# A second visit with plain float32 scores, differences and splits on GpSimd, and free PSUM banks for the last gather

## The chip, the cores and the metric

The kernel runs on one core of a Trainium2 chip. TensorE (PE) multiplies matrices into PSUM; VectorE (DVE), ScalarE (ACT) and GpSimd (POOL) do elementwise work; SyncE (SP) issues the DMAs. The metric is the device time of one execution in microseconds (us), lower is better, given as the median of several runs. One further execution was taken by the profiler, and all rows come from it.

## What is computed

An attention in which each row sees only the rows of its own hash bucket, and a feed-forward layer on its output:

```python
q_bits = (einsum('bhsd,dk->bhsk', q, proj) > 0)      # 6 bits, k likewise
mask = q_bucket[:, :, :, None] == k_bucket[:, :, None, :]
scores = where(mask, 0.125 * q @ k.T, -1e9)          # B, H, S, D = 4, 8, 768, 64
attn = exp(scores - max) / (sum + 1e-9)
x = (attn @ v).transpose(0, 2, 1, 3).reshape(3072, 512)
out = maximum(x @ w_in, 0) ** 2 @ w_out              # w_in 512x2048, w_out 2048x512
```

## The kernel before, in words

The kernel has a fast and a general version; the fast one runs, checks its own assumptions (`verify`), and the general one is behind a branch that is not taken. All that follows is of the fast one.

Attention is cut into visits: a batch, a pair of heads and one half (384) of the queries. A visit has two times three units of 128 queries. A unit's scores go to PSUM (`pS`), VectorE evacuates them to `e` with the row's maximum, ScalarE takes the exponential with the row's sum, and the reciprocal `rv` of the sum is made from it. In the first four visits GpSimd divides (`e<-e,rv`), TensorE transposes into `pT`, and ScalarE or VectorE copies that to `aT`. In later ones ScalarE and VectorE write a high and a low float16 part (`hl`), and a DMA transposes them. `av` multiplies by the values into `pA`, and `xx` takes its high and low part.

Scores are usually made from operands that are stacked to 128 rows in float16: `prep` loads `R`, takes its high part `A` and low part `L`, and by ten DMAs for a pair of heads (`Q<-A`, `Q<-L`, `A<-A`, `L<-M`, `M<-Q`) stacks those with the hash codes `M`. The first visit does without: `first` and `side_by_side` take the loaded keys `K` and queries `G` in float32 on 64 rows of TensorE, and the codes `MK` and `MG` in float16, for both heads of the pair next to each other. `WIDE = 1` is the number of such visits.

The weights come as float64, are put together to float32 (`top`, `f`), and split into a high and a low float16 part (`win`, `wo`). When the four visits of a batch half are done, `moe` runs for it: eight times, each with 16 slices of the hidden layer. A slice is 12 matmuls into `pm`, a Relu and a square into `g32`, the high part and the difference to it (`left`) into `g`, and 9 matmuls into the three banks of `po`, where all 16 slices are gathered. At the end of a layer the three banks are moved to `o` and stored.

The order on each engine is not that of the code. `Program` notes all operations with their dependencies, and `order` plans forwards and backwards with a cost for each operation, which also decides for operations with several ways (`pr.add`) which engine takes it: the end on that engine plus its cost times `PRICE`. In `forward` a `port` that VectorE and GpSimd share is reserved (`held`) for the operations that the function `port` names. `region` tells which parts of a tile an operation touches; in PSUM that is a bank, and two readings of one bank count as dependent too. The instructions are then issued in the planned order, with semaphores that are set from the tiles.

Of the kernel before, what the change touches and what calls it, by code (L numbers as in the profile page):

```python
# [23 lines left out]
P = 128  # L24
# [14 lines left out]
    True: dict(xx=12, hl=3, f=3, e=4, aT=3, g=2, A=8, Q=8, L=8, M=8, R=2, VV=5),  # L39
    False: dict(xx=12, hl=3, raw=2, f=7, e=3, aT=3, g=2, A=2, Q=2, L=2, M=2, R=2, VV=6),  # L40
}
PRICE = dict(pe=1, dve=3.57, act=0.3, pool=3.06, sp=0.43)
AHEAD, DELAY, LAG = 60, 2500, 1.0

ROUNDS, BEHIND = 4, 40000
# [16 lines left out]

TOP_BY, LOW_BY = ("dve", "act"), ("dve", "pool")
RUN = 18
CONSTS_BY, WIDE = ("sp", "sp", "sp"), 1
CHECK_RANK, EARLY = 200, 24


# [61 lines left out]
class Program:  # L130
# [24 lines left out]
    @staticmethod  # L155
    def region(view):
        ap, rec = view.ap, view.rec
        size = lambda dims: 1 + sum(st * (n - 1) for st, n in dims)
        if rec.kind == "dram":
            return 0, 1, ap.offset, ap.offset + size(ap.ap), 0, 0, 0  # L160
        p0, f0 = divmod(ap.offset, rec.row)
        if rec.kind == "psum":
            return 0, 1, f0 // 512, 1 + (f0 % rec.row + size(ap.ap[1:]) - 1) // 512, 0, 0, 0

        (step, n), inner = ap.ap[1], size(ap.ap[2:])
        block = (step, f0 % step, f0 % step + inner) if n > 1 and f0 % step + inner <= step else (0, 0, 0)
        return (p0, p0 + ap.ap[0][1], f0, f0 + size(ap.ap[1:])) + block

    def add(self, *ways):


        ways = [w for w in ways if w[0].key != "pool" or not any(isinstance(x, View) and x.rec.kind == "psum" for x in w[2])]
        queue, name, args, kw = ways[0]
        if name == "matmuls":
            used = [(x, n == 0) for a, _ in args for n, x in enumerate(a)]
        else:
            used = [(args[0], True)] + [(x, False) for x in args[1:]] + [(x, k == "accum_out") for k, x in kw.items()]
        used = [(x.rec, w, self.region(x)) for x, w in used if isinstance(x, View)]
        i, deps = len(self.ops), set()
        for rec, w, (p0, p1, f0, f1, fs, g0, g1) in used:  # L180
            if rec.before is not None:
                deps |= rec.before.ops
            for j, w2, (a0, a1, b0, b1, bs, c0, c1) in rec.accesses:
                if (w or w2 or rec.kind == "psum") and a0 < p1 and p0 < a1 and b0 < f1 and f0 < b1 and not (fs and fs == bs and (c1 <= g0 or g1 <= c0)):
                    deps.add(j)
        for rec, w, r in used:
            rec.ops.add(i)
            rec.accesses.append((i, w, r))
        deps.discard(i)
        if self.mark is not None:  # L190
            self.paced.append((i, self.mark))
        self.ops.append(Op([w + (self.cost(w[0].key, *w[1:]), self.port(w[0].key, *w[1:])) for w in ways], deps, self.rank))

    @staticmethod
    def cost(key, name, args, kw):
# [3 lines left out]
        if name == "matmuls":  # L199

            side = {32: 4, 64: 2}.get(size(args[0][0][1]), 1)
            t = sum(size(a[2]) * column.get(a[2].dtype, 1 / 2.4) + 7 for a, _ in args) / side
            return t, t
        kinds = [x.rec.kind if isinstance(x, View) else "" for x in args]
        ptr = any(isinstance(x, View) and x.shape[-1] == 1 for x in args[2:3])
# [29 lines left out]
    def port(key, name, args, kw):  # L235
# [4 lines left out]
        inside = all(x.rec.kind == "sb" for x in ins)  # L240
        if key == "pool":
            return any(x.rec.kind == "sb" for x in args[1:] if isinstance(x, View) and len(x.shape) > 1 and x.shape[-1] > 1)
        return inside and (len(ins) == 2 or name in ("tensor_copy", "tensor_scalar"))

    def order(self):
        ops = self.ops
# [71 lines left out]
    def forward(self, prio, near):  # L318
# [5 lines left out]
        later = {k: [] for k in keys}  # L324
        ready = {k: [] for k in keys}
        free = dict.fromkeys(keys, 0.0)
        out, dma, dge, held, kind = [], 0.0, 0.0, 0.0, None

        def offer(i):
            for w in ops[i].ways:  # L330
# [8 lines left out]
        while True:  # L339
# [44 lines left out]
            if o.name.startswith("dma"):  # L384
# [4 lines left out]
                    o.busy = busy = dma + 467 - t  # L389
                dma += done  # L390
                done = dma + 910 - t
            free[k], o.end = t + busy, t + done
            out.append(i)
            for j in o.users:
# [54 lines left out]
def run(ctx: ExitStack, tc, kq, v, proj2, w_in, w_out, consts, out, flag):  # L449
# [56 lines left out]
    if fast:  # L506
# [5 lines left out]
        dve.memset(masks[T, 1:2], -65504.0)  # L512
        dve.memset(masks[U, 0:1], 2.0**16)
        dve.memset(masks[U, 1:2], 0.0)
        codes = sb([P, 4 * P], BF16, "codes")
        for t, x in enumerate((2.0 / BIG, 2.0)):
            for j in range(2):
                w = slice(2 * j, 2 * j + 2)
# [288 lines left out]
    def moe(n, b, half):  # L807
# [6 lines left out]
        for f in range(NF + 1):  # L814
# [23 lines left out]
            if f > 0:  # L838
# [2 lines left out]
                pr.mark = None  # L841
                first, last = (m % 4 == 0, m % 4 == 3) if grouped else (m == 0, m == NF - 1)
                if first:
                    po = ps([P, 3, DM], F32, "po")
                for t in range(3):
                    gh = g[:, 0, t * P : (t + 1) * P]
                    gl = g[:, 1, t * P : (t + 1) * P]
                    pr.rank, pr.mark = RANK_PE, pace()
                    pe.matmul(po[:, t], gh, wo[:, 0, m], start=first, stop=False)
                    pe.matmul(po[:, t], gh, wo[:, 1, m], start=False, stop=False)  # L850
                    pe.matmul(po[:, t], gl, wo[:, 0, m], start=False, stop=last)
                    pr.mark = None
                pr.rank = RANK_MOE
                if grouped and last:
# [3 lines left out]
                for t in range(3):  # L858
                    r0 = b * S + half * HS + t * P
                    if grouped and last:  # L860
                        if m == 3:
                            move(acc[:, t], po[:, t], back)
                        else:
                            dve.scalar_tensor_tensor(acc[:, t], po[:, t], back, acc[:, t], ALU.mult, ALU.add)
                        if m == NF - 1:
                            send(out[r0 : r0 + P], acc[:, t])
                    elif last:
                        o = sb([P, DM], F32, "o", tag="f")
                        move(o, po[:, t], back)
                        send(out[r0 : r0 + P], o)  # L870
            if n == 0 and f in (1, 5, 9):
                j = f // 4 + FIRST
# [160 lines left out]
```

## Time and profile before

| | |
|---|---|
| median of 3 runs | 832.88 us (832.54 to 834.76) |
| the profiled execution | 834.86 us, span 833.1 us |
| TensorE busy | 794.3 us (95%) |
| ScalarE busy | 656.6 us (79%) |
| VectorE busy | 605.2 us (73%) |
| GpSimd busy | 72.7 us (9%) |
| DMA, share of 16 engines | 77.2% |

A row of a timeline gives the start and the duration in us, the engine, the line, the operation with output and inputs by the program's names, and the shapes; in brackets the idle time of the engine just before, and what ended it. A matmul's duration holds its latency, so that the steps between starts tell what TensorE gets through. Every operation goes through one helper line, so all rows have L427 or L424, and names tell them apart.

### The profile page before, as it was taken

How to read it: one execution, taken by the hardware profiler on the slowest of the kernel's cores; microseconds unless marked ns; L12 is line 12 of the kernel's file. 1: busy time of each engine (PE TensorE's matmuls, PEld its weight loads, DVE VectorE, ACT ScalarE, POOL GpSimd, SP SyncE). 2: the span in 40 equal slices, each digit the busy share in tenths (PEclk: the TensorE clock that was granted, in tenths of full speed). 3: DMA queues.
4: the chain of work that ended last, by engine and by line, in shares of the span. 5: the costliest groups of instructions: out<-in, count | busy, mean ns of one | idle time of the engine just before them, and what ended most of it. 6: DMA issues, size and time to landing. Idle time of an engine off the chain costs nothing. (4 is left out here: it accounts for less than half of the span.)

```text
span 833.1 us, 14383 instructions
## 1 busy us (share of the span) xinstructions
PE 794.3 (95%) x5001; PEld 430.0 (52%) x5001; DVE 605.2 (73%) x1200; ACT 656.6 (79%) x1238; POOL 72.7 (9%) x175
## 2 busy tenths in 40 slices
PE   7797799999999999999999999999999999999996
PEld 4354355555555554555555545555555554555553
DVE  6888989998999888898879755888889433611110
ACT  5898999998888989888898856888988997334443
POOL 1255200100000010000000000000002000000000
PEclk9999999999999999999999999999999999999999
DMA  8985979999999999999989866988975889501001
GB/s 258 270 223 181 292 188 179 214 176 195 183 202 196 195 188 213 192 181 219 194 188 186 212 165 140 181 143 148 146 133 99 239 290 304 212 1 39 1 1 42
DMA packets 299521, 145.93 MB, mean 175 GB/s; under 512 B 268752, under 2 KB 279344, under 8 KB 299440
## 3 DMA queue, kind: packets, MB, share of 16 engines
q1 hardware_dynamic: 299440, 144.93, 77.2%
q8 instruction: 41, 0.67, 0.3%
q14 instruction: 40, 0.33, 0.1%
HBM read 56.80 MB, written 6.29 MB: 76 GB/s over the span
## 5 line engine op out<-in xcount | busy, mean ns | idle before, releaser
L427 PE MATMUL po<-wo,g 128*128 128x512 f16 x1152 | 296.9, 379 | 5.7 <-ACT o L427 5.7
L427 PE MATMUL pm<-xx,win 128*128 128x384 f16 x1536 | 297.7, 326 | 4.4 <-ACT g L427 2.8
L427 PEld LDWEIGHTS <-win 128*128 128x128 f16 x1536 | 149.9, 98 | 116.6 <-issue 8.0
L427 DVE TENSOR_SCALAR_CACHE_REDUCE e<-pS 128x768 f32<-128x768 f32 x192 | 182.7, 953 | 21.9 <-PE pS L427 17.7
L427 ACT ACTIVATE e<-e,maxes 128x768 f32<-128x768 f32 x192 | 178.2, 929 | 20.7 <-DVE e L427 19.2
L427 DVE SCALAR_TENSOR_TENSOR hl<-e,rv,hl 128x768 f16<-128x768 f32 x168 | 171.0, 1019 | 18.8 <-ACT hl L427 17.8
L427 PEld LDWEIGHTS <-g 128*128 128x128 f16 x1152 | 111.9, 98 | 124.8 <-issue 9.1
L427 ACT ACTIVATE hl<-e,rv 128x768 f16<-128x768 f32 x168 | 154.6, 923 | 6.0 <-DMA aT<-hl 5.2
L427 DVE SCALAR_TENSOR_TENSOR g<-g,g 128x384 f16<-128x384 f32 x121 | 66.9, 553 | 111.8 <-ACT g L427 111.4
L427 ACT ACTIVATE g<-g 128x384 f32<-128x384 f32 (+1 forms) x251 | 129.4, 517 | 6.6 <-PE po L427 2.7
L427 ACT ACTIVATE g<-pm 128x384 f32<-128x384 f32 x127 | 61.2, 482 | 90.3 <-PE pm L427 90.0
L427 PE MATMUL pS<-A,Q 128*128 128x384 f16 x372 | 93.1, 330 | 4.1 <-DVE e L427 2.6
L427 PE MATMUL pS<-L,M 128*128 128x384 f16 x372 | 91.8, 327 | 0.8 <-DMA M<-Q 0.8
L424 PE MATMUL pA<-aT,VV 128*64 128x384 f16 x1008 | 87.2, 327 | 0.0
L427 POOL TENSOR_SCALAR rv<-sums 128x1 f32<-128x1 f32 x136 | 36.8, 271 | 541.7 <-ACT e L427 400.2
L424 PEld LDWEIGHTS <-VV 128*64 128x64 f16 x1008 | 54.7, 110 | 32.9 <-issue 10.0
L427 PEld LDWEIGHTS <-Q 128*128 128x128 f16 x372 | 34.2, 98 | 43.1 <-issue 16.2
L427 DVE TENSOR_SCALAR M<-pc,masks 128x384 f16<-128x384 f32 x64 | 43.0, 672 | 15.4 <-PE pc L427 15.2
L427 PEld LDWEIGHTS <-M 128*128 128x128 f16 x372 | 36.3, 98 | 25.1 <-DMA M<-Q 1.2
L427 ACT ACTIVATION_READ_ACCUMULATOR e<-e,maxes 128x1 f32 x192 | 36.6, 191 | 0.0
L427 DVE SCALAR_TENSOR_TENSOR L<-R,A 128x768 f16<-128x768 f32 x32 | 30.4, 950 | 7.7 <-ACT A L427 7.5
L427 PE MATMUL pT<-unit_f,e 128*128 128x128 f32 x144 | 23.8, 293 | 10.5 <-ACT aT L427 7.7
(82 smaller groups left out, 517.4 us busy)
## 6 DMA issues: line engine op xcount, KB each, us to landing
R<-kq SPq DMA_DIRECT2D x32, 384.0 KB, 3.8
X<-kq SPq DMA_DIRECT2D x32, 384.0 KB, 4.1
raw<-w_in SPq DMA_DIRECT2D x16, 511.8 KB, 5.6
raw<-w_out SPq DMA_DIRECT2D x16, 511.8 KB, 4.9
V<-vp SPq DMA_DIRECT2D x20, 384.0 KB, 5.1
out<-o SPq DMA_DIRECT2D x24, 256.0 KB, 2.7
X<-vp SPq DMA_DIRECT2D x16, 384.0 KB, 4.4
Q<-L SPq DMA_DIRECT2D x32, 96.0 KB, 2.9
```

What stands on the lines that cost most here:

```text
L424: ins = q.engine.matmul(*map(real, args), **kw).ins
L427: ins = getattr(q.engine, o.name)(*map(real, o.args), **{k: real(x) for k, x in o.kw.items()}).ins
```

## The change

- `WIDE = 2`: the first visits of two head pairs use `first` and `side_by_side`. Their stacked operands are needed only for the other query half, four visits later.
- `PRICE` of ScalarE goes from 0.3 to 1, of GpSimd from 3.06 to 1.5, so GpSimd gets more of what it may take: differences, splits and high parts.
- The function `port` names for VectorE only `tensor_copy` and `tensor_scalar` inside SBUF, no longer operations with two SBUF inputs.
- The planner takes a PSUM tile as one region, and two readings as independent.
- The planner knows of eight DMA lanes (`LANES`): SP waits for the DMA eight before.
- TensorE's side-by-side products get a cost of their own.
- In the last of the eight layers `po` is two banks of the tile `pS` and one of `pA`, and the middle `o` of each layer is VectorE's.
- `codes` shares buffers with `g32`.

```diff
-PRICE = dict(pe=1, dve=3.57, act=0.3, pool=3.06, sp=0.43)
+PRICE = dict(pe=1, dve=3.57, act=1, pool=1.5, sp=0.43)
...
+LANES = 8
-CONSTS_BY, WIDE = ("sp", "sp", "sp"), 1
+CONSTS_BY, WIDE = ("sp", "sp", "sp"), 2
...
         if rec.kind == "psum":
-            return 0, 1, f0 // 512, 1 + (f0 % rec.row + size(ap.ap[1:]) - 1) // 512, 0, 0, 0
+            return 0, 1, 0, 1, 0, 0, 0
...
-                if (w or w2 or rec.kind == "psum") and a0 < p1 and p0 < a1 and b0 < f1 and f0 < b1 and not (fs and fs == bs and (c1 <= g0 or g1 <= c0)):
+                if (w or w2) and a0 < p1 and p0 < a1 and b0 < f1 and f0 < b1 and not (fs and fs == bs and (c1 <= g0 or g1 <= c0)):
...
             t = sum(size(a[2]) * column.get(a[2].dtype, 1 / 2.4) + 7 for a, _ in args) / side
+            if args[0][0][1].shape[0] == D and len(args) == 2:
+                t *= 0.5 if args[0][0][2].dtype == F32 else 0.7
...
-        return inside and (len(ins) == 2 or name in ("tensor_copy", "tensor_scalar"))
+        return inside and name in ("tensor_copy", "tensor_scalar")
...
                 done = dma + 910 - t
+                if k != "pool":
+                    lanes.append(t + done)
+                    if len(lanes) >= LANES:
+                        busy = max(busy, lanes[-LANES] + 60 - t)
...
-        codes = sb([P, 4 * P], BF16, "codes")
+        codes = sb([P, 4 * P], BF16, "codes", 2, tag="g32")
...
                 if first:
-                    po = ps([P, 3, DM], F32, "po")
+                    if fast and n == 2 * B - 1:
+                        po = ps([P, 2, 512], F32, "pS"), ps([P, 512], F32, "pA")
+                        po = [po[0][:, 0], po[0][:, 1], po[1]]
+                    else:
+                        po = ps([P, 3, DM], F32, "po")
+                        po = [po[:, t] for t in range(3)]
...
-                        move(o, po[:, t], back)
+                        move(o, po[t], back, (dve,) if fast and t == 1 else (act, dve, pool))
```

The order of instructions changes everywhere. Three places show how. First GpSimd's queue at the start, before: the sums' `rv` and the divisions of the first visit.

```order
L427 TENSOR_SCALAR rv_257<-sums_244 128x1 [waits Activation_49]
L427 TENSOR_SCALAR e_232<-e_232,rv_257 128x768 [waits DVE_49]
L427 TENSOR_SCALAR rv_283<-sums_244 128x1 [waits Activation_49]
L427 TENSOR_SCALAR e_246<-e_246,rv_283 128x768 [waits DVE_49]
L427 TENSOR_SCALAR rv_338<-sums_244 128x1 [waits Activation_49]
L427 TENSOR_SCALAR e_301<-e_301,rv_338 128x768 [waits DVE_49]
```

And the same place after:

```order
L434 TENSOR_SCALAR rv_198<-sums_192 128x1 [waits Activation_49]
L434 TENSOR_SCALAR e_184<-e_184,rv_198 128x768 [waits DVE_49]
L434 TENSOR_TENSOR win_201<-f_187,win_201 128x512 [waits Activation_49]
L434 TENSOR_SCALAR rv_246<-sums_192 128x1 [waits Activation_49]
L434 TENSOR_TENSOR win_201<-f_203,win_201 128x512 [waits Activation_49]
L434 TENSOR_TENSOR L_269<-R_144,A_251 128x768 [waits DMAHW4_49,Activation_49]
L434 TENSOR_SCALAR A_280<-R_190 128x768 [waits DMAHW2_49]
L434 TENSOR_SCALAR e_195<-e_195,rv_246 128x768 [waits DVE_49]
L434 TENSOR_SCALAR e_255<-e_255,rv_278 128x768 [waits DVE_49,Activation_49]
```

Between the first and the second division there are now two low parts of `w_in`, an `L` and an `A`.

Second, SP's queue, before, from its 17th entry: the first visit's `K` and `G` and the second's `R` are issued, and the stacking of the second visit begins (`Q_189`, `Q_221`).

```order
L427 DMA Q_189<-L_140 64x768 [waits DMAHW1_49,DVE_49]
L427 DMA R_195<-kq 128x768 [waits DMAHW2_49,PE_49,Activation_49]
L427 DMA Q_189<-A_97 64x768 [waits DMAHW3_49]
L427 DMA R_216<-kq 128x768 [waits DMAHW4_49,DVE_49,PE_49]
L427 DMA Q_221<-L_191 64x768 [waits DMAHW5_49]
L427 DMA Q_221<-A_173 64x768 [waits DMAHW6_49]
```

And after, from the 11th entry: the second visit's `K_157` and `G_165`, with the third visit's `R` around them.

```order
L434 DMA R_144<-kq 128x768 [waits DMAHW4_49]
L434 DMA unit_f_149<-consts 128x128 [waits DMAHW5_49]
L434 DMA K_157<-kq 64x768 [waits DMAHW6_49]
L434 DMA K_157<-kq 64x768 [waits DMAHW7_49]
L434 DMA G_165<-kq 64x384 [waits DMAHW0_49]
L434 DMA G_165<-kq 64x384 [waits DMAHW1_49]
L434 DMA R_190<-kq 128x768 [waits DMAHW2_49]
```

The second visit has four plain loads and no stacking; the first stacking DMA is ten entries later in the queue.

Third, TensorE at the end of the last layer, before: the gather of the last two slices, in one tile `po`.

```order
L427 MATMUL po_8985<-wo_460,g_9387 128x512
L427 LDWEIGHTS g_9365
L427 MATMUL po_8985<-wo_460,g_9365 128x512 [waits Activation_49]
L427 LDWEIGHTS g_9387
L427 MATMUL po_8985<-wo_460,g_9387 128x512
L427 LDWEIGHTS g_9387
L427 MATMUL po_8985<-wo_460,g_9387 128x512 [waits Activation_49]
```

And after, in the tiles `pS` and `pA`:

```order
L434 LDWEIGHTS g_9394
L434 MATMUL pS_8992<-wo_386,g_9394 128x512
L434 LDWEIGHTS g_9384
L434 MATMUL pA_9003<-wo_386,g_9384 128x512
L434 LDWEIGHTS g_9384
L434 MATMUL pA_9003<-wo_386,g_9384 128x512
L434 LDWEIGHTS g_9394
L434 MATMUL pA_9003<-wo_386,g_9394 128x512
```

The two waits for ScalarE's evacuations are gone from TensorE's queue; five matmuls into `pA` follow the last one into `pS`.

## Rows read from the trace of the kernel before

**Rows 1.** Busy us (x instructions) per engine in four stretches, then clock, DMA, GB/s.
```profile
0.00:97.70 97.70, 74.65 (x485) 43.33 (x485) 79.60 (x175) 80.62 (x162) 36.09 (x53) 0.97 0.83 242
97.70:655.00 557.30, 551.63 (x3586) 299.11 (x3586) 480.87 (x948) 481.71 (x878) 36.65 (x122) 1.00 0.90 181
655.00:819.00 164.00, 161.41 (x902) 84.62 (x900) 43.59 (x76) 90.37 (x193) 0.00 (x0) 1.00 0.39 126
819.00:833.10 14.10, 6.61 (x33) 2.92 (x30) 1.12 (x2) 3.88 (x8) 0.00 (x0) 0.86 0.17 62
```

**Rows 2.** TensorE's waits in 0 to 97.7: us in total, times, longest.
```profile
PE pT L427 <- ACT aT L427: 7.7, 8, 2.2
PE pc L427 <- ACT bits L427: 3.0, 2, 2.8
...
PE pS L427 <- DMA A<-A: 1.3, 1, 1.3
...
PE pS L427 <- DMA M<-Q: 0.8, 1, 0.8
```

**Rows 3.** TensorE's waits from 97.7 on.
```profile
PE po L427 <- ACT o L427: 5.7, 8, 0.9
PE pm L427 <- ACT g L427: 2.8, 5, 1.0
```

**Rows 4.** Timeline where the first stage ends, GpSimd and TensorE.
```profile
89.62 0.91 POOL L427 TENSOR_SCALAR e<-e,rv 128x768 f32<-128x768 f32 x1 [3.42 <-PE pT L427]
...
97.70 0.32 PE L427 MATMUL pm<-xx,win 128*128 128x384 f16 x1 [1.04 <-ACT xx L427]
```

**Rows 5.** Timeline of TensorE in the first visit.
```profile
6.78 1.55 PE L424 MATMUL pS<-K,G 64*128 64x384 f32 x4
...
22.14 1.56 PE L424 MATMUL pS<-K,G 64*128 64x384 f32 x8
23.53 0.49 PE L424 MATMUL pS<-MK,MG 64*128 64x384 f16 x4
23.95 0.85 PE L424 MATMUL pd<-R,pj 128*32 128x384 f32 x8
```

**Rows 6.** The chain that ended last: start us, us, what, in steps.
```profile
628.92 0.65 PE pS L427 x4
629.74 1.73 PE po L427 x8
```

**Rows 7.** By tile (`e`, `f`, `g`, `hl`): duration ns min/median/max, first and last start.
```profile
L427 POOL TENSOR_SCALAR e<-e,rv x24: 907/909/1468, 17.0 to 89.6; 128x768 f32<-128x768 f32 x24
...
L427 DVE SCALAR_TENSOR_TENSOR f<-raw,top x22: 671/684/876, 13.2 to 95.9; 128x512 uint32<-128x512 uint32 x22
...
L427 POOL TENSOR_TENSOR g<-g,g x7: 912/915/1041, 147.0 to 644.1; 128x384 f16<-128x384 f32 x7
...
L427 DVE SCALAR_TENSOR_TENSOR hl<-e,rv,hl x168: 998/1015/1706, 115.4 to 653.6; 128x768 f16<-128x768 f32 x168
```

**Rows 8.** Groups by form: busy us, mean ns of one, idle before and its releaser.
```profile
L427 DVE SCALAR_TENSOR_TENSOR L<-R,A 128x768 f16<-128x768 f32 x32 | 30.4, 950 | 7.7 <-ACT A L427 7.5
...
L427 POOL TENSOR_TENSOR win<-f,win 128x512 f16<-128x512 f32 x3 | 3.5, 1173 | 4.1 <-ACT win L427 4.0
```

**Rows 9.** Timeline of GpSimd and VectorE at 639.8.
```profile
639.80 0.92 POOL L427 TENSOR_TENSOR g<-g,g 128x384 f16<-128x384 f32 x1 [2.70 <-ACT g L427]
639.83 1.71 DVE L427 SCALAR_TENSOR_TENSOR hl<-e,rv,hl 128x768 f16<-128x768 f32 x1
```

**Rows 10.** Timeline of the end, TensorE and ScalarE.
```profile
824.90 0.81 PE L427 MATMUL po<-wo,g 128*128 128x512 f16 x3 [0.69 <-ACT o L427]
...
826.39 0.59 PE L427 MATMUL po<-wo,g 128*128 128x512 f16 x2 [0.69 <-ACT o L427]
827.02 0.60 ACT L427 ACTIVATE o<-po 128x512 f32<-128x512 f32 x1 [0.68 <-PE po L427]
```

**Rows 11.** Timeline of one slice in the last layer.
```profile
805.94 0.33 PE L427 MATMUL pm<-xx,win 128*128 128x384 f16 x1
...
807.94 0.56 DVE L427 SCALAR_TENSOR_TENSOR g<-g,g 128x384 f16<-128x384 f32 x1 [3.33 <-ACT g L427]
```

More of the change, by code (lines that the diff above doesn't have):

```diff
@@ L326, in forward @@
         free = dict.fromkeys(keys, 0.0)
-        out, dma, dge, held, kind = [], 0.0, 0.0, 0.0, None
+        out, dma, dge, held, kind, lanes = [], 0.0, 0.0, 0.0, None, []
         def offer(i):
@@ L848, in moe @@
                     pr.rank, pr.mark = RANK_PE, pace()
-                    pe.matmul(po[:, t], gh, wo[:, 0, m], start=first, stop=False)
-                    pe.matmul(po[:, t], gh, wo[:, 1, m], start=False, stop=False)
-                    pe.matmul(po[:, t], gl, wo[:, 0, m], start=False, stop=last)
+                    pe.matmul(po[t], gh, wo[:, 0, m], start=first, stop=False)
+                    pe.matmul(po[t], gh, wo[:, 1, m], start=False, stop=False)
+                    pe.matmul(po[t], gl, wo[:, 0, m], start=False, stop=last)
                     pr.mark = None
@@ L861, in moe @@
                         if m == 3:
-                            move(acc[:, t], po[:, t], back)
+                            move(acc[:, t], po[t], back)
                         else:
-                            dve.scalar_tensor_tensor(acc[:, t], po[:, t], back, acc[:, t], ALU.mult, ALU.add)
+                            dve.scalar_tensor_tensor(acc[:, t], po[t], back, acc[:, t], ALU.mult, ALU.add)
                         if m == NF - 1:
```

## The prediction

> **What bounds the kernel now.** I first read the busy time of the engines in four stretches [rows 1], because the share over the whole span averages stages with different limits. From 97.7 us on TensorE is busy 551.6 of 557.3 us and then 161.4 of 164.0 us: whatever other engines gain there is worth nothing unless a wait of TensorE goes. In the first 97.7 us it is busy 74.7 us, so 23 us are lost, while ScalarE (80.6) and VectorE (79.6) are the full ones and GpSimd (36.1) is not. That stretch ends when the fourth visit's attention output lets the first feed-forward matmul start, at 97.70 [rows 4]. Next come the waits of TensorE. Early ones are for the copies of transposed weights, for bits and for the DMAs that stack the second visit's operands [rows 2]; after 97.7 us the largest single item is `po` behind ScalarE's `o`, 5.7 us in 8 waits, then 2.8 us for `g` [rows 3]. So the time is: end of the first stage, plus TensorE's remaining work, plus its stalls, plus the end. The change is worth what it does to these four terms.
>
> **First stage, the second visit.** It gets float32 scores on 64 rows instead of stacked float16. Removed ahead of it: two of the four `pc` products, and the stacking DMAs for which TensorE waited 1.3 and 0.8 us; 3.0 us went to bits that stood before its scores in the queue [rows 2]. I count 4 of these 5.1 us as gained, 0 to 5.1 as bounds. Added to TensorE: a pair of units side by side took 1.81 us (22.14 to 23.95 [rows 5]), against 8 x 0.163 = 1.30 us for stacked ones [rows 6], 0.5 us each for two pairs. The visit's first pair runs one half after the other: four products at 1.55 / 2 us [rows 5] and four small ones at about 0.16 are 3.7 us, 2.4 us more. With three more `pd` (under 0.85 us, the four of [rows 5]) and three `pc` (0.163 each) that is 4.7 us. Its cover is the 23 us of idle TensorE; without the cover it costs all 4.7. Four new loads go on the SP queue and stand before the loads of the third visit; the stacking itself is not gone, it moves behind the fourth visit, where the same ten DMAs and M evacuations are issued.
>
> **First stage, GpSimd's share.** By program order, up to its 24th and last division GpSimd does 24 divisions and 4 low parts before, and now 24 divisions, 15 low parts, 6 `L` differences, 4 `A`, 1 `VV` and 10 high parts. Prices: division 0.909 [rows 7], low part 1.17 [rows 8]; an `L` is not in the trace, and from 0.915 us at 384 and 1.17 at 512 elements [rows 7, 8] the line goes to 1.67 at 768; high parts 0.909 x 512/768 = 0.61. That is 26.5 us before and 21.8 + 17.6 + 10.0 + 4.5 + 6.1 = 60.0 us after. VectorE's operations with two inputs in SBUF up to its fourth `xx`: before 22 `f`, 17 low parts (0.684 each [rows 7]), 8 `L` and 3 `VV` (0.95 [rows 8]), 37.1 us; after 26 `f`, 7 low parts, 2 `L`, 3 `VV`, 27.3 us. These two sums belong together, since such operations do not overlap: with GpSimd's difference at 639.80 running for 0.92 us, VectorE's `hl` of normally 1.015 us took 1.71 [rows 9, 7]. The pair ended after 1.74 us instead of the 1.94 us of its parts, 10% less. The port that they share thus has (26.5 + 37.1) x 0.9 = 57 us of work before, in the 77.3 us from the first `f` at 13.2 [rows 7] to the end of the last division, 89.62 + 0.91 [rows 4]; after, 87.3 x 0.9 = 78.6 us. So ScalarE and VectorE are relieved, but this port becomes full. At 95% of use, which I choose because TensorE, whose order is planned in the same way, keeps 99% where it is full [rows 1], it takes 82.7 us, 5.5 us more; less the 4 us above, +1.5 us. Bounds: -6 (two vector engines relieved, port no limit) to +10 (no overlap in pairs at all).
> The Trainium skill ("SBUF — State Buffer", Who interferes with whom) says that a VectorE instruction with two SBUF inputs and a GpSimd instruction that reads SBUF block each other wholly, whoever is first having the port. The row agrees but for the 0.2 us. By the row the port has 78.6 us of work, by the rule alone 87.3, and +1.5 would be +10.7.
>
> **What is left after it.** At the first feed-forward matmul the new order has one more unit's scores (4 x 0.163) and one more `pd` set (0.85 [rows 5]) behind it: 1.5 us less to follow.
>
> **Evacuations of the gather.** Before, in seven of the eight layers a later bank's matmul stands behind ScalarE's `o` of an earlier one, 0.69 us in the two waits of the last layer [rows 10]. In the new order no such wait stands inside a layer: all matmuls precede the first evacuation or use the other tile. Between layers 2.4 us or more of other matmuls (priced by [rows 6]) cover a chain of three evacuations of some 0.6 us [rows 10]; the last layer, where only 1.5 us stand there, gathers in banks that are free. I take 5.0 of the 5.7 us, bounds 3.0 to 5.7. In the end the last matmuls go to `pA` while two `o` are moved, and the last `o` and its store stay as they are.
>
> **Differences on GpSimd.** 117 `g` differences go from 0.56 us [rows 11] to 0.915 [rows 7]. In the last layers the difference starts at 807.94, 2.0 us after the last `pm` at 805.94 [rows 11], and would end at 808.9; the matmul that needs it stands 3.5 us of matmuls (12 `pm`, 7 `po` [rows 6]) behind, at 809.6: covered, and 0.7 us is left. Between 97.7 and 655 us the same distance is 4.5 to 6.8 us in the middle, but there VectorE's `hl` and `e` share the port: GpSimd's about 156 us in 557 meet 168 `hl` in some 47 places, at half of the 0.7 us of [rows 9] each, 16 us of delay on one of the two engines. Slack should take most: 1.5 us, bounds 0 to 8. Behind a late `hl` is the next `e` on VectorE, and behind that TensorE's `pS`.
>
> **Sum.** +1.5 - 1.5 - 5.0 + 1.5 = -3.5 us. The profiled execution took 834.86 us with a span of 833.1; it is 2 us over the median of 832.88, so I apply the difference to the median: 829.4 us. Its own bounds are 825 to 834.
>
> **Rivals.** First, the relief is real and the port is not the limit: the two full engines of the first stage lose about 8 us (VectorE: 6 `L` and 10 low parts less, 4 `f` and some `rv` more), and the stage ends 6 us earlier instead of 1.5 later: 822 us. For it speaks that GpSimd was idle for 62% of the stage; against it the pair in [rows 9]. Second, slower: the port binds fully. 87.3 us with no overlap at 95% use are 92 us in place of 77.3, less 4: +10.7 instead of +1.5, giving 839 us. It decides once demand on the port exceeds the 77 us; the new planner no longer sets the port aside for VectorE operations with two inputs, so nothing in the order avoids such meetings. The Trainium skill's rule ("SBUF — State Buffer", Who interferes with whom), taken literally, is this case. Third, GpSimd's differences come too late in the long stretch: half of the 16 us reaches TensorE, 8 instead of 1.5, 836 us; for it speak `rv` and `L` ahead of `g` in GpSimd's queue, against it the 4.5 us of distance. That the free banks change nothing, because the waits are replaced by others of the same length, is the low end of that term (3.0) and leaves 831.
>
> **Numbers.** Forecast 0.45, first rival 0.2, second 0.22, third 0.13. A measurement of this kernel can tell about 0.3% (2.5 us) from no change: faster means under 830.4, slower over 835.4. The forecast's span splits into 0.28 faster, 0.16 same, 0.01 slower, the third rival into 0.07 and 0.06; with the others faster 0.48, same 0.23, slower 0.29. The range 820 to 840 holds the forecast's own bounds, both middles of the first two rivals and all but their far halves.
>
> **What would show it.** The first `pm` near 99 us (92 in the first rival, 108 in the second); divisions on GpSimd well above 0.91 us in the mean; the wait of `po` for `o` under 1 us in total; `hl` well above 1.02 us in the mean, with few waits of TensorE for `g` or `e` after the first stage. I am wrong if GpSimd's slower `L` delays the third visit's stacks, if ScalarE is the stage's limit whatever the port does, or if TensorE's idle stretches early on bring the half clock, which the first stage showed only in part (0.97 [rows 1]).

## The result and the profile after

The changed kernel takes 842.17 us (839.84 to 848.23, 6 runs) against 833.05 us: 1.0121 times as long, 95% interval 1.0088 to 1.0154. The forecast was 829.4 with a range to 840; the second rival, the shared port, had named 839. The profiled execution of after took 848.23 us (span 846.4), the longest of its six; its difference to the profiled execution before is 13.3 us, that of the medians 9.1. Steps below are told on the profiled ones, of which there is one for each kernel, verdicts on the medians.

By stages (the columns of [rows 1]), cut at the first `pm`, which is at 109.00 now:

```profile
0.00:109.00 109.00, 91.32 (x506) 48.73 (x506) 84.52 (x176) 80.78 (x158) 80.28 (x84) 0.95 0.82 239
109.00:655.00 546.00, 537.24 (x3492) 290.45 (x3491) 430.74 (x819) 427.26 (x762) 204.64 (x271) 1.00 0.88 176
655.00:819.00 164.00, 162.27 (x912) 85.39 (x911) 39.58 (x75) 98.61 (x204) 39.52 (x48) 1.00 0.50 145
819.00:846.40 27.40, 20.32 (x107) 10.14 (x105) 0.69 (x1) 8.67 (x17) 4.87 (x6) 0.96 0.09 32
```

The first stage is 11.3 us longer (97.70 before), with GpSimd busy for 80 of 109 us where it was for 36 of 98. All that follows takes 737.4 us, where it took 735.4. The relief of the two full engines came: VectorE is busy for 555.5 us instead of 605.2, ScalarE for 615.3 instead of 656.6. The time did not follow.

The same rows show something else. Up to the first `pm` TensorE is busy for 91.32 us, where it was for 74.65 [rows 1], and its idle time there fell from 23.1 to 17.7 us. So the longer stage is not a stage in which TensorE waits longer; TensorE works 16.7 us more. Part of that is its clock. From 5 to 20 us the changed kernel and then the one before:

```profile
5.00:20.00 15.00, 14.71 (x63) 7.46 (x63) 5.45 (x15) 5.53 (x10) 1.58 (x3) 1.00 0.79 240
5.00:20.00 15.00, 13.69 (x102) 7.96 (x99) 11.00 (x25) 8.73 (x15) 1.78 (x4) 1.00 0.95 286
```

TensorE gets through 63 products instead of 102 (fillers that nobody reads among them), and VectorE through 15 operations instead of 25. Four of the same products, early and later in the changed kernel:

```profile
13.87 2.92 PE L431 MATMUL pS<-K,G 64*128 64x384 f32 x4
32.86 1.55 PE L431 MATMUL pS<-K,G 64*128 64x384 f32 x4
```

One lasts up to 1.006 us until 20.5 us, and 0.482 us at 32.86: TensorE was at the lower of its two levels (1.2 and 2.4 GHz) until then, though the clock column of the rows gives 1.00. In the kernel before, four take 1.55 us already at 6.78 [rows 5].

TensorE's waits from 109 us on (total, times, longest), beside [rows 3]:

```profile
PE pS L434 <- DVE e L434: 7.8, 14, 1.5
PE pm L434 <- ACT g L434: 1.3, 1, 1.3
PE pA L431 <- DVE xx L434: 0.3, 1, 0.3
PE pt L434 <- DVE grade L434: 0.2, 1, 0.2
PE po L434 <- POOL g L434: 0.2, 1, 0.2
```

The 5.7 us behind `o` are gone, and 7.8 us behind VectorE's `e` stand in their place: 9.8 us in all, 10.3 before.

By tile (duration min/median/max, first and last start), beside [rows 7]:

```profile
L434 POOL TENSOR_SCALAR e<-e,rv x24: 898/1185/2117, 18.6 to 99.1; 128x768 f32<-128x768 f32 x24
...
L434 DVE SCALAR_TENSOR_TENSOR f<-raw,top x32: 672/884/2148, 15.3 to 123.7; 128x512 uint32<-128x512 uint32 x32
...
L434 POOL TENSOR_TENSOR L<-R,A x26: 1641/1649/2375, 22.8 to 555.1; 128x768 f16<-128x768 f32 x26
L434 DVE SCALAR_TENSOR_TENSOR L<-R,A x6: 1177/1644/2390, 25.4 to 496.6; 128x768 f16<-128x768 f32 x6
...
L434 DVE SCALAR_TENSOR_TENSOR hl<-e,rv,hl x168: 993/1017/2248, 120.2 to 703.0; 128x768 f16<-128x768 f32 x168
```

The shortest ones of `e`, `f` and `hl` are as before; the median division went from 0.909 to 1.185 us, the median `f` from 0.684 to 0.884. One place of the timeline shows how (start, duration):

```profile
62.53 1.65 POOL L434 TENSOR_TENSOR L<-R,A 128x768 f16<-128x768 f32 x1
62.60 2.39 DVE L434 SCALAR_TENSOR_TENSOR L<-R,A 128x768 f16<-128x768 f32 x1
64.17 3.43 POOL L434 TENSOR_SCALAR e<-e,rv 128x768 f32<-128x768 f32 x2
```

VectorE's `L`, 0.95 us before [rows 8], begins 0.07 us after GpSimd's and ends at 64.99, 0.8 us after GpSimd's end at 64.18: it stood still until then. GpSimd's two divisions, 1.82 us of work, then take 3.43, since they stand behind VectorE in turn. The Trainium skill ("SBUF — State Buffer", Who interferes with whom) has the later of the two blocked wholly; this place agrees but for about 0.14 us of overlap.

How full the port was I worked out from each trace: every GpSimd instruction but `rv` and memset, and every VectorE instruction with two SBUF inputs, that begins between the first `f` and the end of the last division, each taken at the shortest duration of its group. The columns for TensorE go up to the first `pm`; "low" is the time at the lower of its two levels, counted from its first product to the first full grant in the trace and over the grants of half the clock.

| kernel | median us | first `pm` | window us | work on the port us | share | TensorE busy us | idle us | low us |
|---|---|---|---|---|---|---|---|---|
| before | 833 | 97.7 | 77.3 | 56.0 | 0.72 | 74.6 | 23.1 | 10.3 |
| after | 842.2 | 109.0 | 84.8 | 83.1 | 0.98 | 91.3 | 17.7 | 28.7 |
| old prices (first run) | 842.5 | 98.1 | 73.8 | 56.0 | 0.76 | 80.2 | 17.9 | 7.8 |
| one visit | 841.7 | 105.2 | 80.8 | 77.9 | 0.96 | 79.9 | 25.3 | 16.9 |
| banks alone | 830.3 | 94.5 | 70.3 | 53.2 | 0.76 | 77.3 | 17.2 | 12.0 |
| 32 idle reads | 855.7 | 113.7 | 91.3 | 81.5 | 0.89 | 82.6 | 31.1 | 21.6 |
| 32 idle writes | 841.4 | 104.9 | 83.8 | 56.7 | 0.68 | 78.4 | 26.6 | 10.7 |
| 16 idle reads | 838.3 | 100.4 | 78.5 | 69.0 | 0.88 | 80.2 | 20.1 | 17.3 |
| 16 idle writes | 836.8 | 98.1 | 74.4 | 56.5 | 0.76 | 78.7 | 19.4 | 11.9 |
| old prices and old rule | 831.3 | 98.8 | 77.2 | 58.6 | 0.76 | 80.8 | 18.0 | 10.6 |
| rule alone | 838.3 | 107.4 | 83.2 | 64.2 | 0.77 | 86.6 | 20.7 | 26.1 |
| prices alone | 835.4 | 100.9 | 81.3 | 73.3 | 0.90 | 78.3 | 22.6 | 7.9 |
| rule taken back | 847.0 | 108.0 | 78.5 | 69.4 | 0.88 | 89.2 | 18.8 | 27.8 |
| before, other plan | 836.3 | 100.9 | 79.6 | 56.4 | 0.71 | 79.6 | 21.3 | 13.8 |
| after, other plan | 840.6 | 105.8 | 84.2 | 77.7 | 0.92 | 85.5 | 20.2 | 18.3 |
| banks, other plan | 829.8 | 101.3 | 74.1 | 58.2 | 0.78 | 78.4 | 23.0 | 15.9 |

The four kernels with 77 us or more on the port have their first `pm` at 105.2 us or later, but three with 57 to 69 us (32 idle writes, the rule alone, the rule taken back) have theirs at 104.9 to 108.0. And a late first `pm` need not cost time: the banks alone have theirs at 94.5 and 101.3 in two plans, at the same 830 us.

### The profile page after: what moved, and what is told of

The parts are those of the page before. It is cut to its first block, busy times and chain, and to the rows that moved or that the text cites. A ratio compares the mean times of both kernels' runs of the same rounds, so it can differ in the third digit from the quotient of the medians.

```text
span 846.4 us, 14483 instructions
## 1 busy us (share of the span) xinstructions
PE 811.1 (96%) x5010; PEld 434.7 (51%) x5010; DVE 555.5 (66%) x1069; ACT 615.3 (73%) x1140; POOL 329.3 (39%) x408
## 5 line engine op out<-in xcount | busy, mean ns | idle before, releaser
L434 PE MATMUL pm<-xx,win 128*128 128x384 f16 x1536 | 310.3, 326 | 1.8 <-ACT g L434 1.3
L434 PE MATMUL po<-wo,g 128*128 128x512 f16 x1008 | 278.0, 379 | 0.3 <-POOL g L434 0.2
L434 DVE SCALAR_TENSOR_TENSOR hl<-e,rv,hl 128x768 f16<-128x768 f32 x168 | 185.8, 1106 | 44.7 <-ACT hl L434 42.3
L434 POOL TENSOR_TENSOR g<-g,g 128x384 f16<-128x384 f32 x124 | 117.0, 944 | 173.1 <-ACT g L434 147.8
L434 ACT ACTIVATE hl<-e,rv 128x768 f16<-128x768 f32 x156 | 144.5, 926 | 12.5 <-DMA aT<-hl 7.1
L434 ACT ACTIVATE g<-g 128x384 f32<-128x384 f32 (+1 forms) x195 | 101.4, 521 | 8.5 <-DVE g L434 3.4
L434 PE MATMUL pS<-A,Q 128*128 128x384 f16 x360 | 90.4, 327 | 12.8 <-DVE e L434 12.8
L434 POOL TENSOR_SCALAR g<-g 128x384 f16<-128x384 f32 x59 | 35.3, 598 | 153.3 <-ACT g L434 117.2
L431 PE MATMUL pA<-aT,VV 128*64 128x384 f16 x1008 | 87.2, 327 | 0.3 <-DVE xx L434 0.3
L434 POOL TENSOR_TENSOR L<-R,A 128x768 f16<-128x768 f32 x26 | 45.2, 1742 | 16.5 <-ACT A L434 15.6
```

Source lines behind the costliest of these rows:

```text
L431: ins = q.engine.matmul(*map(real, args), **kw).ins
L434: ins = getattr(q.engine, o.name)(*map(real, o.args), **{k: real(x) for k, x in o.kw.items()}).ins
```

## The experiments

**Parts undone or done alone.** Theory: the port makes the first stage late. Rival: the second visit's float32 products do.

```diff
-PRICE = dict(pe=1, dve=3.57, act=1, pool=1.5, sp=0.43)
+PRICE = dict(pe=1, dve=3.57, act=0.3, pool=3.06, sp=0.43)
```

> The changed kernel with the old engine prices alone, so that GpSimd has its 24 divisions and only a handful of splits and differences again (in the first stage 1 low part of w_in, 3 of w_out, 1 L). Port theory (what lengthens the first stage, and makes VectorE's evacuation late afterwards, is VectorE and GpSimd shutting each other out): first pm at 97 to 100 us instead of 109, VectorE's f back at about 0.70 us and hl at 1.02 us, TensorE's 7.8 us of waits for e after the first stage down to about 1, time 826 to 830. Wide theory (the second visit's float32 scores, on TensorE and at half clock, lengthen the stage): first pm still at 106 or later, time 835 to 840.

842.45 us, ratio 1.0115 (1.0085 to 1.0145). Half of the theory held, half fell. With GpSimd's share gone the first `pm` is at 98.1, `hl` at 1.014 us and the median `f` at 0.688. But the time did not follow and lies outside both expectations: after the first `pm` this kernel takes 739.6 us in its profile, with 12.0 us of waits, these ahead:

```profile
PE pm L434 <- ACT xx L434: 4.1, 2, 2.2
PE pS L434 <- DVE e L434: 2.6, 4, 1.3
PE po L434 <- DVE g L434: 2.0, 3, 1.2
PE pm L434 <- ACT g L434: 1.6, 3, 0.8
```

Another part of the change must cost, too.

```diff
-CONSTS_BY, WIDE = ("sp", "sp", "sp"), 2
+CONSTS_BY, WIDE = ("sp", "sp", "sp"), 1
...
             if args[0][0][1].shape[0] == D and len(args) == 2:
-                t *= 0.5 if args[0][0][2].dtype == F32 else 0.7
+                pass
```

> The changed kernel with one visit on float32 scores, as before; GpSimd keeps its new work. Port theory: the first pm stays at 106 to 111 us and the time at 839 to 845. Wide theory: first pm at 98 to 100, time 831 to 834.

841.73 us, 1.0125 (1.0100 to 1.0149), first `pm` at 105.2: as the port theory had it. Undoing the visit alone gains nothing. Its first `pm` is 3.8 us earlier in this pair of profiles, but that is no price of the visit: here TensorE's products are at the upper level from the first `K`, `G` at 6.3 us, in the changed kernel only behind 20.5.

```diff
-                left(g[:, 1], g32, 1.0, g[:, 0])
+                dve.scalar_tensor_tensor(g[:, 1], g32, 1.0, g[:, 0], ALU.mult, ALU.subtract)
```

> The changed kernel with the differences g of the feed-forward layer fixed to VectorE (0.55 us each there, 117 of them come back from GpSimd); the first stage keeps GpSimd's new work. If GpSimd's differences cause the late evacuations of the long stretch: first pm still near 109, but TensorE's waits for e after it fall from 7.8 to 1 or 2 us, time 835 to 837. If they are harmless and the waits come from the new order: 7 us of such waits stay, time 841 to 844.

849.42 us, 1.0183 (1.0153 to 1.0214): outside both expectations. First `pm` at 110.9; waits for `e` still 4.8 us, and 4.9 new ones of `po` for VectorE's `g`. GpSimd's differences were at most a part of what held `e` up; with them back on VectorE the kernel is 7 us slower than the changed one by the medians, 0.6% by the ratios.

The kernel before with the new code for `po` and `o` and the PSUM regions, all else old:

```diff
+                    if fast and n == 2 * B - 1:
+                        po = ps([P, 2, 512], F32, "pS"), ps([P, 512], F32, "pA")
...
+                        move(o, po[t], back, (dve,) if fast and t == 1 else (act, dve, pool))
```

> The kernel before with the free banks of the last layer, the PSUM tile as one region and the middle o on VectorE alone; no second float32 visit, old prices, old port rule. If the 5.7 us of waits for o are a gain of their own: those waits under 1 us, first pm at 97 to 98.5, time 826 to 829. If other waits take their place: 831 to 834, with 4 to 5 us of new waits of TensorE after the first stage.

830.29 us, 0.9969 (0.9957 to 0.9982). The waits for `o` fall from 5.7 to 0.5 us, and little takes their place. The first `pm` is 3.2 us earlier besides, but in another plan of the same kernel 3.6 us later (below), so that is not the banks'. The waits:

```profile
PE pm L434 <- ACT g L434: 2.1, 3, 1.2
PE pS L434 <- DVE e L434: 1.4, 4, 0.4
PE pm L434 <- ACT xx L434: 1.0, 1, 1.0
PE po L434 <- ACT o L434: 0.5, 1, 0.5
```

**The port by itself.** Two kernels with the same order on all engines; they differ in what 32 idle GpSimd instructions do. `extra` is called behind each low part of `w_in`, and the planner counts its instructions as taking no time.

```diff
+    def extra(low):
+        spare, fours = wo[:, 1, NF - 1], unit_f.unsqueeze(1).broadcast_to([P, 4, P])
+        for _ in range(2):
+            pool.tensor_tensor(spare.rearrange("p (a b) -> p a b", a=4), fours, fours, ALU.subtract)
+            o = pr.ops[-1]
+            o.deps.add(low)
+            o.ways = [w[:4] + ((0, 0), False) for w in o.ways]
```

> The kernel before with 32 more GpSimd instructions in the first stage, whose result nobody needs: after each low part of w_in two tensor_tensor that read SBUF (128x512, the form of the low parts, some 1.17 us each, 37 us in all). All else is planned as if they took no time. Port theory (VectorE's operations with two SBUF inputs and GpSimd's reading ones shut each other out): f and L on VectorE grow from 0.70 and 0.95 us to over 0.9 and 1.3, first pm at 103 to 110 us, time 838 to 844. Queue theory (GpSimd's own queue is what makes the divisions late): the same lateness, but VectorE's durations stay. If GpSimd's added work as such is harmless: first pm at 96 to 99, time 831 to 835.

855.65 us, 1.0284 (1.0258 to 1.0310), first `pm` at 113.7: far more than either theory had. And the writing ones, `pool.memset(wo[:, 1, NF - 2 :], 0.0)` in place of the `tensor_tensor`:

> The same kernel with the same order on every engine, but the 32 idle GpSimd instructions are memsets of 128x1024 float16, which read nothing. Port theory: f and L on VectorE stay near 0.70 and 0.95 us and the first pm is earlier than with the reading ones by 5 us or more, near 97 to 100, time 831 to 836. Queue theory: the first pm as late as with the reading ones, as far as a memset lasts as long.

841.44 us, 1.0129 (1.0100 to 1.0157), first `pm` at 104.9, more than the port theory had. The groups (busy us, mean ns | idle before), of the reading kernel and then of the writing one:

```profile
L427 POOL TENSOR_TENSOR wo<-unit_f 128x512 f16<-128x512 f32 x32 | 40.2, 1256 | 16.0 <-DMA unit_f<-consts 14.1
...
L427 DVE SCALAR_TENSOR_TENSOR f<-raw,top 128x512 uint32<-128x512 uint32 x32 | 30.0, 940 | 1.9 <-ACT top L427 1.9
L427 POOL TENSOR_SCALAR e<-e,rv 128x768 f32<-128x768 f32 x24 | 28.0, 1173 | 5.1 <-DVE rv L427 2.6 <-PE pT L427 1.1 <-ACT A L427 0.8
```

```profile
L427 POOL MEMSET wo<- 128x1024 f16 x32 | 30.6, 956 | 1.7 <-POOLq L1036 0.3
...
L427 POOL TENSOR_SCALAR e<-e,rv 128x768 f32<-128x768 f32 x24 | 26.7, 1116 | 18.7 <-DVE rv L427 17.8 <-PE pT L427 0.4
L427 DVE SCALAR_TENSOR_TENSOR f<-raw,top 128x512 uint32<-128x512 uint32 x32 | 22.5, 705 | 3.2 <-ACT top L427 3.2
```

14.2 us lie between them, in the profiles 8.8 up to the first `pm` and 4.8 behind it. An undisturbed one of the reading instructions lasts 1.04 us (at 76.24):

```profile
76.24 1.04 POOL L427 TENSOR_TENSOR wo<-unit_f 128x512 f16<-128x512 f32 x1
```

So the queue of the reading kernel is longer by 32 x 0.09 = 3 us; the other 11 us come from the reading, and VectorE's `f` shows where: 0.940 us against 0.705. With memsets it is untouched. That is the port. Up to the first `pm` TensorE waits 4.5 us longer with the reads (31.1 against 26.6), and it works 4.2 us longer, at its lower level for 21.6 us instead of 10.7: in this pair a longer wait and a lower clock came together. But the writing kernel, too, is 9.4 us over before. That fits the queue theory, by which a division that stands behind idle work is late without any port, but it is not shown: the kernel before has another order, and an order alone moved the time by 3.5 us (below). The Trainium skill ("SBUF — State Buffer", Who interferes with whom) says that a GpSimd instruction that only writes SBUF doesn't meet VectorE's two inputs; these runs agree.

Half the dose, `range(1)`, again one order for both:

> The kernel before with 16 instead of 32 idle GpSimd instructions that read SBUF, one after each low part of w_in, about 19 us. Full-port view of the prediction: 0.9 x (26.5 + 37.1 + 19) = 74 us of work on the port in 77 us, so the first pm at 97 to 100 and 832 to 835 us. If each meeting costs at once: half of the 16 us that 32 of them cost, first pm at 104 to 107, 842 to 846.

> The same order with 16 idle memsets in place of the 16 reading ones. If reading is what costs, earlier than the reading ones by 4 to 8 us (half of the 14 us between the two kernels with 32): 834 to 838. If it is only the time in GpSimd's queue: within 3 us of the reading ones.

838.31 us (1.0065, 1.0048 to 1.0083) with reads and 836.82 us (1.0045, 1.0029 to 1.0061) with writes; first `pm` at 100.4 and 98.1. The time with reads lies between its two expectations, since already the writes cost 4 us, little more than another plan does (below). Reading itself costs 1.5 us at half the dose, 14.2 at the full one. For half the dose that is what GpSimd's queue alone was expected to give (within 3 us), and not the 4 to 8 us of a price for each meeting. The prediction's sum would explain both doses: 69.0 us of work against a window of 77 before, then 81.5. It does not explain the rule alone (below), which has less work on the port and a first `pm` at 107.4.

**The long stretch.** The kernel with the banks, and `pool.tensor_tensor(g[:, 1], g32, g[:, 0], ALU.subtract)` for `left`:

> The kernel before with the free banks, and the 122 remaining differences g fixed to GpSimd; the first stage has the old shares and one float32 visit. It does in the long stretch what the change does there, without its first stage. If GpSimd's differences cost there: hl above 1.08 us in the mean, 5 to 8 us of waits of TensorE for e or g after the first pm, time 835 to 838 against 830.3 with them on VectorE. If they are harmless or help: 828 to 831.

829.76 us, 0.9985 (0.9968 to 1.0003), against 830.29 us, 0.9969, without. Harmless within the noise: `g` takes 0.988 us on GpSimd and `hl` 1.036, and TensorE waits 1.2 us for `e` and 0.3 for `g` after the first `pm`.

**The visit and the rule.** The changed kernel with old prices and old `port` rule:

> The changed kernel with the old engine prices and the old port rule: the second float32 visit and the free banks stay, GpSimd's shares are those of before. Beside the kernel with the banks alone (830.3 us) it prices the second visit. If the visit is worth what the prediction took (4 us of waits gone, covered by idle TensorE): first pm at 91 to 94, time 826 to 829. If the float32 products cost what they take on TensorE: first pm at 97 to 99, time 833 to 837. If it stays at the 842 us that the old prices alone gave, the port rule has no part in that.

831.32 us, 1.0007 (0.9981 to 1.0033), between two expectations: 1.0 us more than the banks alone by the medians, 0.4% by the ratios. First `pm` at 98.8 against 94.5 there. The cost of the side-by-side products, `LANES` and the shared buffers of `codes` are in this kernel too, so they cost no more than that together with the visit, as long as prices and rule are old. This kernel differs from the first one in a single line, the rule, and that one took 842.45.

```diff
-        return inside and (len(ins) == 2 or name in ("tensor_copy", "tensor_scalar"))
+        return inside and name in ("tensor_copy", "tensor_scalar")
```

This line alone, in the kernel before:

> The kernel before with the new port rule alone, one line. GpSimd's share stays small (24 divisions, 5 low parts, 11 differences). If the 11 us between the old and the new rule at old prices are the rule's own: 840 to 846, with VectorE's and GpSimd's operations stretched about twice as much by meetings as before. If they came from the rule together with the second visit: 832 to 835.

838.32 us, 1.0077 (1.0057 to 1.0097), between the two expectations; first `pm` at 107.4 in its profile, median `f` 0.693 but mean 0.811. The operations on the port, 64.2 us of work, took 81.3 us, where before 56.0 took 61.0: the meetings stretch them, though the port has room. With the 16 idle reads they were stretched as much (69.0 to 87.2 us) and cost 1.5 us more than the writes, so the stretch alone does not decide either. TensorE is at its lower level for 26.1 us up to the first `pm`, 10.3 before. The new prices alone:

> The kernel before with the new prices alone, the old port rule kept: GpSimd takes 16 low parts of w_in, all L and all differences. By program order it has some 60 us of work in the first stage as after the change. If the rule is what costs: 830 to 834. If the share of work on GpSimd costs by itself, through its slower L (1.7 us against 0.95) and its queue: first pm at 103 to 108, 838 to 843.

835.38 us, 1.0043 (1.0026 to 1.0060), again between the two, first `pm` at 100.9: with 73.3 us of work on the port by the table's count, and a planner that knows of it, the stage is 3 us longer. The change with only the rule taken back:

> The changed kernel with the old port rule alone: GpSimd keeps most of its new share (14 low parts of w_in, 8 L, 128 differences), but the planner sets the port aside for VectorE's operations with two SBUF inputs again. So far, with the second visit and the banks: old prices and old rule 831.3 us, old prices and new rule 842.5, new prices and new rule 842.2. If the planner's blindness to the port is the cause: f near 0.75 us and hl near 1.03, 829 to 834. If GpSimd's share of the first stage is too much work for the port even when planned for: first pm at 104 to 110, 838 to 844.

846.96 us, 1.0198 (1.0165 to 1.0230): slower than both expectations and than the change itself, and against the view that the rule alone is to blame. Its first `f` is at 19.6 instead of 15.3, and its first `pm` at 108.0. TensorE's granted clock up to there is 0.89 in its profile, the lowest in the clock column of all these kernels; why the plan brings that is not settled. Then the rule with the differences on GpSimd:

> The kernel with free banks and the differences on GpSimd (829.8 us) with the new port rule added. If the rule, by which the planner no longer keeps VectorE's hl and GpSimd's g apart, makes the stalls: hl at 1.08 us or more in the mean, 5 us or more of waits for e after the first pm, 838 to 844. If the rule matters in the first stage only: few such waits, time 832 to 837 through a later first pm. If neither: 829 to 832.

836.25 us, 1.0043 (1.0029 to 1.0057): the second expectation; first `pm` at 103.3 against 98.7, and 2.5 us of waits for `e` afterwards.

**Plans.** Each of these kernels has another order. What that does alone, `AHEAD` 90 instead of 60 in the kernel before:

> The kernel before with the planner's horizon for shares at 90 instead of 60: the same work, another order in detail. It shows what a plan costs or gains by itself: 830 to 835 if plans of the same work differ little, 836 or more if the plan of before is a lucky one, so that part of every edit's loss is no more than that.

836.31 us, 1.0048 (1.0030 to 1.0067). The plan of before is a good one; a single edit that costs or gains less than some 4 us says little. Two kernels with `LAG` 1.05 instead of 1:

> The changed kernel with the planner's lags between engines 5% longer: the same edits, another order (GpSimd 14 low parts of w_in, 5 L, 24 divisions in the first stage). If the loss is the port's, which any plan with such shares meets: first pm at 104 to 112, 839 to 850. If the loss was one bad plan: 830 to 836.

> The kernel with the free banks alone (830.3 us), planned with the same 5% longer lags. The gain that is the banks' own is in TensorE's waits for o: under 1 us again in place of 5 to 6. The time 828 to 836, by the plan; under 832 would say that the banks gain more than plans differ.

The change in another order takes 840.60 us (1.0089, 1.0063 to 1.0115), with its first `pm` at 105.8; the banks alone take 829.78 (0.9940, 0.9921 to 0.9960), with theirs at 101.3 and the waits for `o` at 0.3 us. Loss and gain outlive a new plan, the place of the first `pm` does not. The kernel with the free banks beats both kernels of this case in both plans.

## Why the prediction was wrong

*The first stage* (+1.5 forecast, +11.3 measured in the two profiles) is the step that failed, and in it the 4 us taken off for the second visit, whose products idle TensorE was to cover. The stage parts at the first `f` and at the end of the last division: 2.1 us more ahead of the window (first `f` at 15.3 against 13.2), 7.5 more in it, 1.8 more behind it.

- The port, forecast +5.5: the window is 84.8 us instead of 77.3, +7.5. Like with like, 87.3 us of work were forecast before the overlap and 83.1 counted; with it 78.6 us at 95% use, and the operations on the port cover 76.5 us of the window, 90%. The sum was nearly right, 2.0 us too small. (Its 82.7 less 77.3 is 5.4, and GpSimd was idle for 63% of the stage, not 62; neither matters.) Its `L` of 1.67 us on GpSimd measured 1.65.
- The second visit, forecast -4: outside the window the stage got 3.8 us longer. Of the 5.1 us of waits in [rows 2] that were counted 1.5 are left. But TensorE's added work was put at 4.7 us and covered by 23 us of idle time; it is 16.7 us, and the idle time gave 5.4 of them, from 23.1 to 17.7. About 6 us of it would be the visit's: the old prices with either rule, with two visits as well, have TensorE busy for 80.2 and 80.8 us.

```profile
0.00:98.10 98.10, 80.24 (x503) 43.12 (x503) 84.37 (x181) 81.89 (x165) 43.81 (x52) 0.98 0.84 248
```

There the cover held: with about 18 us of idle time the first `pm` is at 98.1 and 98.8, about where it was before.

- TensorE's clock had no term. The prediction named it among the signs of being wrong ("if TensorE's idle stretches early on bring the half clock"), and the record shows it: 28.7 us at the lower level up to the first `pm`, where it was 10.3. If half of that time is work not done, that is 14.3 us instead of 5.2, an estimate from these two counts. The 48 `pS<-K,G` products show it, in the changed kernel and then with the old prices:

```profile
L431 PE MATMUL pS<-K,G 64*128 64x384 f32 x48 | 18.4, 648 | 0.4 <-DVE e L434 0.4
L431 PE MATMUL pS<-K,G 64*128 64x384 f32 x48 | 14.5, 531 | 0.0
```

No run tells how much of the +11.3 is the port's and how much the clock's. Both go up together in the changed kernel. The prices alone have much work on the port and little time at the lower level (73.3 and 7.9 us, first `pm` at 100.9), the rule alone has the reverse (64.2 and 26.1, at 107.4). Nor is it known how much belongs to this one execution, which is 6 us over the median of the changed kernel: in the other plan of the same change TensorE is at the upper level from 7.6 us on, and the first `pm` comes at 105.8.

What the visit costs by itself is not shown. With old prices and old rule its first `pm` at 98.8 lies between the 94.5 and the 101.3 of two plans without it, and the 109.0 against 105.2 with GpSimd's new share holds the late clock. In the medians it costs 1.0 us without the new shares (0.4% by the ratios) and 0.4 us with them (nothing by the ratios).

Behind the first `pm` three terms were to give -5.0 us together; that part got 2.0 us longer. *Remaining work* (-1.5): TensorE is busy for 719.8 us after the first `pm`, and for 719.7 before. Nothing was saved.

*The evacuations* (-5.0): the waits went wholly, as predicted, and alone the banks gain 2.4 and 3.8 us in the two pairs of medians, so half to three quarters of the term. In the changed kernel 7.8 us of waits for `e` stand against it.

*GpSimd's differences* (+1.5) were the wrong culprit: alone they cost nothing that the noise lets see. The late `e` of the changed kernel come in part from the weights' splits, which now run on GpSimd until 129 us, under the long stretch. The longest such place:

```profile
126.99 1.21 POOL L434 TENSOR_SCALAR g<-g 128x384 f16<-128x384 f32 x1
128.17 1.15 POOL L434 TENSOR_TENSOR wo<-f,wo 128x512 f16<-128x512 f32 x1
128.23 1.50 DVE L434 SCALAR_TENSOR_TENSOR g<-g,g 128x384 f16<-128x384 f32 x1 [0.41 <-POOL g L434]
129.66 0.94 DVE L434 TENSOR_SCALAR_CACHE_REDUCE e<-pS 128x768 f32<-128x768 f32 x1
130.66 0.48 PE L434 MATMUL pS<-A,Q 128*128 128x384 f16 x2 [1.50 <-DVE e L434]
```

VectorE's difference, 0.55 us as a rule, begins behind a low part of `w_out` on GpSimd and takes 1.50; the evacuation behind it is late, and TensorE waits. That is the chain that the prediction named ("behind a late `hl` is the next `e` on VectorE, and behind that TensorE's `pS`"), with another instruction at its head. What delays the other 13 was not taken apart.

*The rivals.* The second one named the first `pm` at 108 and 839 us, and 109 and 842 came. In good part that was luck. Its window was 92 us, with no overlap in pairs, and it took the same 4 us off; the window is 84.8, nearer to the forecast's 82.7, the 4 us did not come, and the two errors cancel. What spoke for it, a planner that no longer sets the port aside, was in the text with a chance of 0.22, and the rule alone does cost 6.2 us. I took a port that is 95% in use, because TensorE keeps 99% where it is full [rows 1]; it was 90%. As I see it, and no run tests it, TensorE has work of other visits and slices to go on with, while GpSimd's divisions of the first stage stand in one chain from scores to `pm`.

*What stays open.* The parts don't add up: banks -2.4, prices +3.3, rule +6.2, visit +1.0 come to +8.1 of the 9.1 us, but with two visits the rule alone costs 11.1 and the prices alone 15.6, and taking back any one part (visit, prices or rule) gains at most 0.4 us. Each edit makes another plan, and single plans of one work differ by 3.5 us. What is shown, by pairs of one order, is that GpSimd's reads stretch VectorE's operations with two SBUF inputs and that 32 of them cost 14.2 us, some 3 of these through GpSimd's longer queue; and with GpSimd's old share the first `pm` is back at 98.1, though not the time. That the port makes the changed kernel's 9 us, directly or by leaving TensorE idle and at the lower clock, is argued and not shown, and so is how they split between shares and rule.

## What to carry to other kernels

Before work goes to an idle GpSimd, sum what it reads from SBUF together with VectorE's operations of two SBUF inputs, over the stage and not the span: in a stage of 77 us 13 us of added reads were nearly free here, 25 were not, however idle GpSimd looked. The sum is a warning and no measure: a plan with 64 us lost as much of the stage as one with 78. When a stage gets longer, look first whether its fullest engine waits more or works more, and if it works more, at how long the same product takes early and late; here TensorE's busy time grew by 16.7 us where the second visit would account for about 6. And where a planner sets the order, time a second plan of the same work before reading a difference of half a per cent as an edit's effect; and don't take the end of a stage for the time. What held in both plans here was the one edit that only took waits away.

## What the runs showed of the hardware

Memsets of 128x1024 float16 on GpSimd (0.956 us each) left VectorE's operations with two inputs untouched (`f` 0.705 us), while reading ones of like length raised them to 0.940.

In the changed kernel's profile TensorE stayed at its lower level until 20.5 us, though it was busy for 14.71 of the 15 us from 5 on, and a product of `K` and `G` took 1.006 us instead of 0.482; in another plan of the same change it rose at 7.6 us. What decides that, no run here shows.

Not expected either was how much a mere reordering of the same work moves this kernel: 832.80 to 836.31 us, with the first `pm` at 100.9 instead of 97.7; and with the free banks the first `pm` moved from 94.5 to 101.3 us while the time stayed.
